# Decode attention with a small MLP on one core: one load queue, a pinned matrix-engine order, a spread-out MLP and a split query-weight load

## The chip, the cores and the metric

The kernel runs on one core of a Trainium2 chip. The metric is the device time of one execution in microseconds (us). A kernel that was timed several times is given by its median. The profile of one execution is shown beside it; its span, from the first to the last instruction, is 1.7 to 2.6 us (1.8 in the median) shorter than the device time of the same execution.

Engine names: PE is TensorE's matmul, PEld its weight load, DVE is VectorE, ACT is ScalarE, POOL is GpSimd, SP is SyncE, which only issues transfers here. PSUM is the memory that PE writes its results to. A packet is one piece of a transfer as the profile's DMA records list it. The granted clock is TensorE's clock as a share of full speed, as the profile page gives it.

## The reference

One token, 16 query heads, 8 K/V heads, 65,536 cached positions of 256 values in bfloat16. The cache is 537 MB and every byte is used once. A small token-mixing MLP and a sigmoid gate are added.

```python
def _A_ref(x, k_cache, v_cache, wq, wo):        # x: (1, 1, 448)
    q = (x @ wq).reshape(B, Sq, 16, 256)...      # wq: (448, 4096)
    k, v = repeat(k_cache, 2), repeat(v_cache, 2)   # (1, 8, 65536, 256) each
    p = softmax(einsum("bhqd,bhkd->bhqk", q, k) * 256 ** -0.5)
    return einsum("bhqk,bhkd->bhqd", p, v)... @ wo  # wo: (4096, 448)

def _B_ref(x, w1, b1, w2, b2):
    h = _layernorm(x)                            # 448 values
    u = gelu(einsum("bsd,sf->bdf", h, w1) + b1)  # 448 x 1792
    return einsum("bdf,fs->bds", u, w2) + b2

g = sigmoid((x * gate_w).sum(-1))
return g * a + (1 - g) * b
```

## The kernel before

The cache is worked through in 256 chunks of 2,048 positions: 1 MB of K and 1 MB of V each. Position `p*16 + j` lies on partition `p`, so one partition receives 8 KB in one piece. PE transposes K in 32 blocks of 128 by 128, DVE copies them out of PSUM, PE forms the scores, ACT takes the exponential, DVE transposes it, and PE multiplies it with V. There are 4 K buffers and 5 V buffers. A helper library puts the instructions of each engine into an order and inserts the waits.

K and the query weight are issued by SP, V by ACT:

```python
wqT = big.tile([PX, KCX, HQ * DH], BF16)              # 112 partitions, 4 x 4096
nc.sync.dma_start(out=wqT[:], in_=A_wq.rearrange("(p kc) n -> p kc n", kc=KCX))
# ... (the query projection, then the output weight's load by POOL)

for g in range(HKV):
    pending = None
    for ck in range(n_chunks):
        # ... buffers of this chunk
        nc.sync.dma_start(out=kn[:, :, :], in_=k_src)
        nc.scalar.dma_start(out=vt[:, :, :], in_=v_src)
        # ... 4 x (8 transposes into tps, copy to kT)
        # ... 8 score matmuls of this chunk
        if pending is not None:
            pv_matmuls(pv, *pending)                  # the chunk before
        nc.scalar.activation(out=p_sb[:, :], in_=ps[:, :], func=ACT.Exp, ...)
        nc.vector.tensor_tensor(out=denacc[:], in0=denacc[:], in1=den[:], op=ALU.add)
        nc.vector.transpose(out=pT[:, :], in_=p_sb[:, :])
        pending = (pT, vt, (ck == 0), (ck == n_chunks - 1))
    pv_matmuls(pv, *pending)
    if g == 0:
        mixer_mlp()                                   # the whole MLP, after head 0
    # ... finish of the head: normalize, output projection into a_ps
```

The MLP, in 14 blocks (the first layer's matmuls are in float32):

```python
for blk in range(NF):
    nc.tensor.matmul(u_ps, lhsT=w1_row[0:1, blk*128:(blk+1)*128], rhs=h_row[0:1, :], start=True, stop=False)
    nc.tensor.matmul(u_ps, lhsT=b1_row[0:1, blk*128:(blk+1)*128], rhs=ones_f32[0:1, :], start=False, stop=True)
    # ... ACT copy, 4 DVE operations and a Tanh on 128 x 448
    nc.tensor.matmul(y_ps, lhsT=w2T_t[:, blk, :], rhs=gel_blk, start=(blk == 0), stop=(blk == NF - 1))
```

The softmax here doesn't subtract the row's maximum and nothing guards it: scores larger than these inputs give would overflow.

## Time and profile before

| | before |
|---|---|
| time, first 4 runs | 1353.27 us median (1352.37 to 1357.23) |
| span of the profiled execution, mean granted clock | 1352.1 us, 0.933 |
| bytes moved, mean rate | 546.37 MB, 404 GB/s |
| PE, DVE, ACT busy | 73%, 65%, 15% |

How to read it: no engine is busy all the time, but the 16 DMA engines nearly are (90% or more in 38 of the page's 40 slices). 546.37 MB at 420 GB/s take 1301 us. So 51 us of the span are not explained by the bytes, and the question is where the rate falls below 420.

These are lines of the profile page of before. The last two have 40 equal slices of 33.8 us: the granted TensorE clock in tenths of full speed, and the rate of the loads.

```profile
span 1352.1 us, 33043 instructions
...
PEclk9789997999899999998989999998899999999988
...
GB/s 281 397 419 419 419 420 325 358 419 420 420 420 419 420 419 420 419 420 420 419 416 419 413 420 413 418 413 413 420 419 418 417 419 417 420 409 412 419 420 178
```

The rate is 419 or 420 in most slices. It is low in the first two, in slices 7 and 8 (325 and 358), a little in some slices after the twentieth (413, 409), and in the last.

Two lines of the table of waits of before say who waits for the loads (total us, times, longest).

```profile
PEld L295 <- DMA kn<-in_A_k_cache_dram: 326.4, 226, 3.0
...
PE tps L295 <- DMA kn<-in_A_k_cache_dram: 225.2, 178, 2.8
```

PE waits for K some 200 times. The loads are the limit, and engine work matters where it holds buffers back. That is the case at 210 us. The columns of the next windows are: from and to; length; busy us of PE, PEld, DVE, ACT and POOL with instruction counts; granted clock; busy share of the DMA engines; GB/s. The two lines under them are from the groups of instructions (line, engine, operation, shapes, count; busy us, mean ns of one; idle before).

```profile
210.00:220.00 10.00, 10.00 (x50) 4.29 (x48) 7.45 (x16) 2.80 (x7) 0.00 (x0) 0.61 0.94 373
220.00:230.00 10.00, 9.67 (x82) 5.50 (x81) 6.03 (x10) 1.79 (x4) 0.00 (x0) 0.71 0.62 236
230.00:240.00 10.00, 10.00 (x79) 4.67 (x78) 7.67 (x18) 2.80 (x6) 0.00 (x0) 0.66 0.76 284
240.00:250.00 10.00, 8.32 (x114) 5.46 (x111) 8.29 (x17) 1.95 (x5) 0.00 (x0) 1.00 0.79 286
250.00:260.00 10.00, 9.60 (x160) 6.39 (x158) 8.86 (x17) 1.83 (x5) 0.00 (x0) 1.00 0.97 388
```

```profile
L224 PE MATMUL oo_ps<-ones_f,b_row 1*128 1x448 f32 x28 | 16.9, 691 | 0.0
L220 PE MATMUL oo_ps<-h_row,w_row 1*128 1x448 f32 x28 | 16.7, 681 | 0.0
```

The MLP's first layer in before is these 28 float32 matmuls (two per block, each recorded twice, so 56 records) of 0.68 to 0.69 us a record. From 210 to 240 us PE is busy 9.67 to 10.00 of 10 us at a clock of 0.61 to 0.71, SP's next loads wait for PE's transposes to free a K buffer (55.3 us in nine waits from 205 to 260 us, the longest 13.4), and the loads fall to 236 GB/s. The start has another cause. These lines are the DMA issues of before (count, KB of each transfer, median us to landing) and the first windows.

```profile
kn<-in_A_k_cache_dram SPq DMA_DIRECT2D x256, 1024.0 KB, 16.5
wqT<-in_A_wq_dram SPq DMA_DIRECT2D x1, 3584.0 KB
```

```profile
0.00:10.00 10.00, 0.24 (x4) 0.21 (x4) 2.80 (x7) 2.46 (x4) 6.47 (x20) 1.00 0.86 253
10.00:20.00 10.00, 0.00 (x0) 0.00 (x0) 0.93 (x3) 0.52 (x2) 0.00 (x0) 1.00 1.01 249
20.00:30.00 10.00, 3.58 (x129) 3.50 (x129) 0.55 (x4) 0.00 (x0) 1.72 (x1) 1.00 0.92 292
30.00:40.00 10.00, 7.17 (x71) 5.89 (x71) 5.60 (x15) 1.97 (x3) 0.00 (x0) 0.90 1.01 403
```

From 10 to 20 us the DMA share is 1.01 and the rate only 249 GB/s: the DMA engines work, but slowly. The packet records show why: the query weight travels in packets of 32 KB that take 2.1 us each, where a K or V packet of 8 KB takes 0.314 us. Last, the windows of before around the end of the loads:

```profile
1326.00:1330.00 4.00, 3.01 (x44) 2.54 (x45) 1.39 (x3) 0.69 (x2) 0.00 (x0) 0.79 0.92 381
1330.00:1334.00 4.00, 3.71 (x56) 2.44 (x55) 2.80 (x7) 0.58 (x2) 0.00 (x0) 0.79 0.51 205
1334.00:1338.00 4.00, 2.77 (x50) 1.83 (x48) 2.47 (x6) 0.22 (x3) 0.00 (x0) 1.00 0.27 113
```

At 1330 us the DMA share is 0.51 at 205 GB/s: half of the DMA engines have nothing left to do while the other half still load (in the packet records, some 8 packets are in flight in place of 16).

### The profile page before, as it was taken

To read this page: it belongs to the slowest core of one execution; us is meant where nothing else is said; L and a number is where in the kernel's file an instruction comes from. 1 tells how busy PE (TensorE), PEld (TensorE's weight loads), DVE (VectorE), ACT (ScalarE), POOL (GpSimd) and SP (SyncE) were. 2 spreads that over 40 slices of the span, in tenths; PEclk is the share of its full clock that TensorE was granted. 3 is DMA by queue.
4 is the path that set the end of the run, shared out by engine and by line. 5 is a ranking of instruction groups with operands and counts; after the bars stand their busy time and mean duration, and the time that the engine had idled before them with its cause. 6 is when DMAs were issued, how large, how long until landed. Compare 5 with 4: busy or idle time off the path is not lost. (4 is left out here: it accounts for less than half of the span.)

```text
span 1352.1 us, 33043 instructions
## 1 busy us (share of the span) xinstructions
PE 990.4 (73%) x14602; PEld 658.2 (49%) x14602; DVE 877.1 (65%) x1665; ACT 196.7 (15%) x554; POOL 8.2 (1%) x21
## 2 busy tenths in 40 slices
PE   2787789877787677767677676777768767777676
PEld 2454555555454445445455444545545444544443
DVE  1576787866666666666666666666666666666665
ACT  0111122111111111111111111111111111111111
POOL 2000000000000000000000000000000000000000
PEclk9789997999899999998989999998899999999988
DMA  9999998999999999999999999999999999999994
GB/s 281 397 419 419 419 420 325 358 419 420 420 420 419 420 419 420 419 420 420 419 416 419 413 420 413 418 413 413 420 419 418 417 419 417 420 409 412 419 420 178
DMA packets 75281, 546.37 MB, mean 404 GB/s; under 512 B 8657, under 2 KB 8674, under 8 KB 9490
## 3 DMA queue, kind: packets, MB, share of 16 engines
q1 hardware_dynamic: 37250, 272.12, 49.2%
q10 hardware_dynamic: 36864, 268.45, 48.3%
q0 software_dynamic: 1024, 3.69, 0.7%
q8 instruction: 114, 1.87, 0.6%
q14 instruction: 29, 0.24, 0.0%
HBM read 544.22 MB, written 0.00 MB: 403 GB/s over the span
## 5 line engine op out<-in xcount | busy, mean ns | idle before, releaser
L300 DVE COPY kT<-tps 128x1024 bf16<-128x1024 bf16 x1024 | 675.0, 681 | 431.6 <-PE tps L295 424.3
L295 PE MATMUL tps<-ident,kn 128*128 128x128 bf16 x8192 | 648.4, 229 | 329.1 <-DMA kn<-in_A_k_cache_dram 225.2
L295 PEld LDWEIGHTS <-kn 128*128 128x128 bf16 x8192 | 509.8, 103 | 553.0 <-DMA kn<-in_A_k_cache_dram 326.4
L319 ACT ACTIVATE p_sb<-sc_ps 128x512 bf16<-128x512 f32 x256 | 152.9, 597 | 1060.8 <-issue 697.2
L308 PE MATMUL sc_ps<-kT,qT_sb 128*2 128x512 bf16 x2048 | 230.2, 399 | 0.8 <-DVE kT L300 0.6
L260 PE MATMUL pv_ps<-vt,pT 128*2 128x256 bf16 x4096 | 213.1, 291 | 2.5 <-DVE pv_sb L336 1.7
L326 DVE STREAM_TRANSPOSE pT<-p_sb 128x512 bf16<-128x512 bf16 x256 | 179.7, 704 | 0.0
L260 PEld LDWEIGHTS <-pT 128*2 128x2 bf16 x4096 | 93.4, 85 | 47.2 <-DVE pT L326 7.5
L308 PEld LDWEIGHTS <-qT_sb 128*2 128x2 bf16 x2048 | 61.0, 82 | 48.7 <-issue 8.9
L319 ACT ACTIVATION_READ_ACCUMULATOR p_sb<-sc_ps 128x1 f32 x256 | 49.8, 194 | 0.0
L323 DVE TENSOR_TENSOR denacc<-denacc,den 128x1 f32<-128x1 f32 x256 | 38.0, 148 | 5.1 <-ACT p_sb L319 5.1
L224 PE MATMUL oo_ps<-ones_f,b_row 1*128 1x448 f32 x28 | 16.9, 691 | 0.0
L220 PE MATMUL oo_ps<-h_row,w_row 1*128 1x448 f32 x28 | 16.7, 681 | 0.0
L174 PE MATMUL misc_ps<-xT,wqT 112*128 112x1 bf16 x128 | 3.6, 165 | 16.5 <-DMA wqT<-in_A_wq_dram 16.5
L174 PEld LDWEIGHTS <-wqT 112*128 112x128 bf16 x128 | 3.5, 104 | 16.6 <-DMA wqT<-in_A_wq_dram 16.6
L229 ACT COPY u_blk<-oo_ps 128x448 f32<-128x448 f32 x14 | 7.4, 527 | 20.0 <-PE oo_ps L224 11.6
L362 PE MATMUL misc_ps<-wo_sb,oT_sb 128*1 128x448 bf16 x32 | 9.0, 377 | 0.0
L237 ACT ACTIVATE t_blk<-t_blk 128x448 f32<-128x448 f32 x14 | 8.0, 572 | 6.9 <-DVE t_blk L236 5.9
L236 DVE TENSOR_TENSOR t_blk<-t_blk,u_blk 128x448 f32<-128x448 f32 x14 | 8.6, 614 | 0.2
L231 DVE TENSOR_TENSOR t_blk<-u_blk 128x448 f32<-128x448 f32 x14 | 8.6, 611 | 0.2 <-ACT u_blk L229 0.2
L193 DVE BATCH_NORM_STATS2 stats<-xB 1x6 f32<-1x448 f32 x1 | 0.6, 615 | 12.4 <-DMA xB<-in_A_x_dram 12.4
L239 DVE SCALAR_TENSOR_TENSOR gel_blk<-t_blk,u_blk 128x448 bf16<-128x448 f32 x14 | 8.3, 612 | 0.0
(58 smaller groups left out, 66.3 us busy)
## 6 DMA issues: line engine op xcount, KB each, us to landing
vt<-in_A_v_cache_dram ACTq DMA_DIRECT2D x256, 1024.0 KB, 16.2
kn<-in_A_k_cache_dram SPq DMA_DIRECT2D x256, 1024.0 KB, 16.5
wqT<-in_A_wq_dram SPq DMA_DIRECT2D x1, 3584.0 KB
wo_sb<-in_A_wo_dram POOLq DMA_DIRECT2D x1, 3584.0 KB, 44.4
xT<-in_A_x_dram SPq DMA_DIRECT2D x1, 0.9 KB, 3.0
gwT<-in_gate_w_dram SPq DMA_DIRECT2D x1, 0.9 KB, 5.7
xB<-in_A_x_dram POOLq DMA_DIRECT2D x1, 1.8 KB, 12.4
w_row<-in_B_w_dram POOLq DMA_DIRECT2D x1, 7.0 KB, 17.2
```

What stands on the lines that cost most here:

```text
L220: nc.tensor.matmul(u_ps[:, :], lhsT=w1_row[0:1, blk * 128:(blk + 1) * 128], rhs=h_row[0:1, :], start=True, stop=False,)
L224: nc.tensor.matmul(u_ps[:, :], lhsT=b1_row[0:1, blk * 128:(blk + 1) * 128], rhs=ones_f32[0:1, :], start=False, stop=True,)
L231: nc.vector.tensor_tensor(out=t_blk[:], in0=u_blk[:], in1=u_blk[:], op=ALU.mult)
L236: nc.vector.tensor_tensor(out=t_blk[:], in0=t_blk[:], in1=u_blk[:], op=ALU.mult)
L260: nc.tensor.matmul(pv[32 * grp:32 * grp + 2, :], lhsT=pT[:, 32 * bcol:32 * bcol + 2], rhs=vt[:, bcol, :], start=first, stop=last, tile_pos ...
L295: nc.tensor.transpose(tp[:, jj * 128:(jj + 1) * 128], kn[:, j, c * 128:(c + 1) * 128], ident[:, :],)
L300: nc.vector.tensor_copy(out=kT[:, c, j0:j0 + 8, :], in_=tp[:, :].rearrange("p (j n) -> p j n", j=8))
L308: nc.tensor.matmul(ps[32 * a:32 * a + 2, :], lhsT=qT_sb[:, c, 2 * g:2 * g + 2], rhs=rhs, start=(c == 0), stop=(c == 1), tile_position=(0, ...
L319: nc.scalar.activation(out=p_sb[:, :], in_=ps[:, :], func=ACT.Exp, scale=inv_sqrt_dh, accum_out=den[:, 0:1],)
L323: nc.vector.tensor_tensor(out=denacc[:], in0=denacc[:], in1=den[:], op=ALU.add)
L326: nc.vector.transpose(out=pT[:, :], in_=p_sb[:, :])
L362: nc.tensor.matmul(a_ps[:, :], lhsT=oT_sb[:, c, h:h + 1], rhs=wo_sb[:, kc, :], start=first, stop=last,)
```

## The change

The intent: let nothing disturb the loads. (1) The query weight goes in four transfers with rows of 8 KB. (2) V moves to SP's queue behind K, 4 chunks ahead; V gets 6 buffers and the transposed K 3. (3) The loop is rewritten so that PE's order is stated and pinned: transposes of the next chunk, scores of this one, PV of the one before. (4) The MLP's first layer folds weight and bias into one matmul of two rows, and its 14 blocks are spread over the first 112 chunks. Sums that stayed open in PSUM for the whole run are now added up by DVE.

```diff
-NKT = 2
-NVBUF = 5
+NKT = 3
+NVBUF = 6
+PREF = 4
@@ the query weight
-    nc.sync.dma_start(
-        out=wqT[:], in_=A_wq.rearrange("(p kc) n -> p kc n", kc=KCX)
-    )
+    for kc in range(KCX):
+        nc.sync.dma_start(
+            out=wqT[:, kc, :], in_=A_wq.rearrange("(p kc) n -> p kc n", kc=KCX)[:, kc, :]
+        )
@@ the loads of a chunk, now in dma_chunk(n)
-            nc.scalar.dma_start(out=vt[:, :, :], in_=v_src)
+        nc.sync.dma_start(out=vt[:, :, :], in_=v_src)
@@ the MLP's first layer, now in mixer_u(blk); w1b1 holds both rows, the second row of h1 is ones
-                u_ps[:, :], lhsT=w1_row[0:1, ...], rhs=h_row[0:1, :], start=True, stop=False,
-                u_ps[:, :], lhsT=b1_row[0:1, ...], rhs=ones_f32[0:1, :], start=False, stop=True,
+            u_ps[:, :], lhsT=w1b1[0:2, blk * 128:(blk + 1) * 128],
+            rhs=h1[0:2, :], start=True, stop=True,
@@ its second layer, now in mixer_y(blk)
+            start=True, stop=True,
+        nc.vector.tensor_tensor(out=y_acc[:], in0=y_acc[:], in1=y_ps[:, :], op=ALU.add)
@@ the loop
+    for n in range(min(PREF, total_chunks)):
+        dma_chunk(n)
+    transposes(0)
+    gate_and_q()
...
+        with tc.manual_schedule(engines={mybir.EngineType.PE}):
+            for n in range(n0, n1):
+                if n + 1 < total_chunks:
+                    transposes(n + 1)
+                scores(n)
+                if last is not None:
+                    pv_stage(last)
+                softmax_stage(n)
+                if n >= 4 and n % 8 == 4 and n // 8 < NF:
+                    mixer_u(n // 8)
+                if n >= 6 and n % 8 == 6 and n // 8 < NF:
+                    mixer_y(n // 8)
+                last = n
+                if n + PREF < total_chunks:
+                    dma_chunk(n + PREF)
```

## The prediction

> **What bounds the kernel now.** The load stream. The profile page: 546 MB moved, mean 404 GB/s over 1352.1 us, nearly all of the 40 slices at 416 to 420 GB/s; PE busy 73%, DVE 65%, ACT 15%. PE waits for K (326 us in the table of waits). At a steady 419.5 GB/s the bytes take 1302 us, so 50 us is lost (table by stretch, packet records):
>
> - 0 to 25 us: 200 to 300 GB/s with the engines busy. The query weight goes as 32 KB packets of 2.1 us (15.5 GB/s per engine); 8 KB packets take 0.314 us (26 GB/s). Lost with the late first byte: 10 us.
> - 40 to 80 us: 398 GB/s beside the output projection's 4.5 KB packets: 2.4 us.
> - 210 to 260 us: 236 to 388 GB/s, 12.7 us. PE is busy 10.0 of 10 us at a granted clock of 0.61 to 0.71: the MLP's 56 fp32 matmuls (0.69 us each) bunch up, K buffers come free late, the queue starves.
> - End: half of the DMA engines run dry 8 us before the others (200 GB/s, 4 us lost), then 15 us of work follow the last landing.
>
> **What the change does.**
> 1. Query weight in four transfers with 8 KB rows: estimated 7 us saved, on the critical path.
> 2. MLP spread over 112 chunks, first-layer matmuls halved: 19 us of PE work and the pile-up gone, 10 to 12 us saved.
> 3. PE's order pinned, the next chunk's transposes ahead of the scores. From the trace's durations (copy 0.65, eight transposes 0.55, scores 0.64, exp with read 0.8, small transpose 0.7 us) I estimate 4.3 us per chunk at full clock, against 5.0 us for its 2 MB. But MLP blocks add 3.3 us per 8 chunks and each head's finish 5 us of PE waiting in line; there compute and loads are nearly level. I allow 3 us of loss.
> 4. K and V on one queue. [...] microseconds in which one queue alone carried data reach 401 to 451 GB/s; an issue costs 0.33 us against 2.5 us per transfer. Neutral.
> 5. Tail: same finish (8 us from the last PV) plus one 0.6 us addition; only V's last 2.5 us lies behind the last K. Estimated 12.5 us.
>
> **Sum.** First byte 3 + bytes and end skew 1306 + projection 2.4 + residual start 1 + tail 12.5 + MLP allowance 3 = 1328 us. From above: 1353 - 7 - 12 - 2.5 - late dips 1 + 3 = 1333. I predict 1328 us, range 1317 to 1342: faster by over 2% 0.40, within 2% 0.55, slower 0.05.
>
> **What would show it.** About 420 GB/s throughout, with no dip near 210 us; query-weight packets at 0.31 us; the half-speed drain of 8 us at the end.
>
> **What would make it wrong.** One queue slower than two (uniformly below 419 GB/s). Low clock in the first half: [...] this trace grants 0.61 during the MLP[...]. Better if the drain at the end vanishes.

Two passages are cut from this text, and marked: the ground that point 4 gave first, and what a lower clock was feared to do. No term of the sum is cut: it came to 1328 us as it stands.

## More of the kernel before

The next lines, from the page of before, list the DMA queues: packets, MB, and the time that the packets took as a share of 16 engines' span.

```profile
q1 hardware_dynamic: 37250, 272.12, 49.2%
q10 hardware_dynamic: 36864, 268.45, 48.3%
...
q8 instruction: 114, 1.87, 0.6%
```

K is on q1 and V on q10.

## The result, and the profile after

| | before | after |
|---|---|---|
| time, runs on the same chip | 1353.58 us (16 runs, 1349.84 to 1357.23) | 1338.27 us (10 runs, 1337.24 to 1338.97) |
| ratio, 95% interval | 1 | 0.9883 (0.9870 to 0.9895) |
| span of the profiled execution, clock | 1352.1 us, 0.933 | 1334.9 us, 0.957 |
| mean rate | 404 GB/s | 409 GB/s |
| PE, DVE busy | 73%, 65% | 68%, 69% |

A ratio is the mean time of one kernel's runs over the mean of the other's runs in the same rounds, so it is not quite the ratio of the medians. The change gains 1.2%: 1338.27 us lies within the predicted range, 10 us above the predicted 1328.

The same lines of the page as before, now of after (a slice is 33.4 us):

```profile
span 1334.9 us, 32973 instructions
...
PEclk9798998999899989999999999999999999999999
...
GB/s 317 411 420 419 420 420 419 420 419 419 420 419 421 419 419 420 419 419 420 419 409 420 419 417 421 409 420 419 413 420 413 420 420 419 411 414 419 416 419 175
```

The dip in slices 7 and 8 is gone and the first two slices are better (317, 411). The late slices still have their 409 to 414, and the last slice is no better. The queues, and the waits for K, in after:

```profile
q1 hardware_dynamic: 74498, 540.58, 98.3%
...
q8 instruction: 113, 1.85, 0.6%
```

```profile
PEld L184 <- DMA kn<-in_A_k_cache_dram: 338.7, 211, 4.8
PE tps L184 <- DMA kn<-in_A_k_cache_dram: 269.4, 197, 4.3
```

One queue carries everything at the same 419 to 420 GB/s. PE waits for K no less than before (338.7 us, 269.4 us), although the kernel is faster, which would fit that it has less work of its own (PE busy 904 us in place of 990) and reaches the wait earlier. A wait at the limiting resource is no measure of what is lost. The windows of after at the same place, and the group of the MLP's first layer:

```profile
210.00:220.00 10.00, 6.60 (x117) 4.87 (x115) 6.79 (x13) 1.38 (x4) 0.00 (x0) 0.99 1.01 419
220.00:230.00 10.00, 7.77 (x78) 4.75 (x79) 6.96 (x13) 1.80 (x4) 0.00 (x0) 0.67 1.02 421
230.00:240.00 10.00, 8.86 (x139) 6.52 (x132) 7.24 (x14) 1.94 (x6) 0.00 (x0) 0.83 1.01 419
```

```profile
L343 PE MATMUL oo_ps<-h,w1b 2*128 2x448 f32 x28 | 14.3, 590 | 0.0
```

28 records of 0.59 us in place of 56, and the loads stay at 419 to 421 GB/s. The start and the end of after:

```profile
wqT<-in_A_wq_dram SPq DMA_DIRECT2D x4, 896.0 KB, 10.3
```

```profile
10.00:20.00 10.00, 2.50 (x81) 2.34 (x82) 2.75 (x13) 0.20 (x1) 0.00 (x0) 1.00 1.02 281
20.00:30.00 10.00, 7.69 (x124) 6.50 (x120) 5.58 (x10) 0.35 (x1) 1.72 (x1) 1.00 1.01 411
```

```profile
1310.00:1314.00 4.00, 2.31 (x43) 1.53 (x43) 2.92 (x6) 0.69 (x2) 0.00 (x0) 1.00 0.58 240
1314.00:1318.00 4.00, 3.10 (x56) 2.20 (x54) 2.75 (x6) 0.69 (x2) 0.00 (x0) 1.00 0.50 205
1318.00:1322.00 4.00, 1.40 (x23) 1.28 (x24) 1.69 (x3) 0.00 (x0) 0.00 (x0) 1.00 0.35 141
```

The slow start ends some 8 us sooner (411 against 292 GB/s from 20 to 30 us; the packet records below have 28 us against 36). The end has the same shape at 205 GB/s, and lasts longer.

To add this up, the packet records were summed by stretch, and each stretch's bytes were set against 419.8 GB/s, the steady rate. "Lost" is the time of the stretch less the time its bytes take at that rate. The clock of the packet records reads 10.3 to 10.6 us more than the span's, so "60 us" here is about 49.5 us in the windows above. "Drain" is from the moment half of the DMA engines run dry (8 packets in flight in place of 16) to the last packet.

```text
lost us         start  60 to  82 to  275 to  600 to  drain         all   rest of the span
                (-60)   82    275    600    drain  (its length)          (before the first and
                                                                          after the last packet)
before          10.2   1.1   12.7    0.1     5.1    4.9 (8.7)    34.1    16.5
after            6.1   0.1    0.1    0.3     4.7    6.8 (12.4)   18.1    15.3
```

The span fell by 17.2 us: 12.6 at the MLP, 4.1 at the start and 1.0 just after it, 0.2 in the middle and late stretches together, 1.2 outside the loads (the tail after the last packet 2.0 shorter, the first packet 0.8 later), and 1.9 were given back in the drain.

### The profile page after: what moved, and what is told of

The parts are those of the page before. It is cut to its first block, busy times and chain, and to the rows that moved or that the text cites. A ratio compares the mean times of both kernels' runs of the same rounds, so it can differ in the third digit from the quotient of the medians.

```text
span 1334.9 us, 32973 instructions
## 1 busy us (share of the span) xinstructions
PE 904.3 (68%) x14574; PEld 643.2 (48%) x14574; DVE 915.2 (69%) x1689; ACT 198.2 (15%) x554; POOL 8.2 (1%) x21
## 5 line engine op out<-in xcount | busy, mean ns | idle before, releaser
L184 PE MATMUL tps<-ident,kn 128*128 128x128 bf16 x8192 | 609.6, 226 | 394.8 <-DMA kn<-in_A_k_cache_dram 269.4
L189 DVE COPY kT<-tps 128x1024 bf16<-128x1024 bf16 x1024 | 662.2, 684 | 210.8 <-PE tps L184 187.6
L184 PEld LDWEIGHTS <-kn 128*128 128x128 bf16 x8192 | 505.4, 101 | 535.0 <-DMA kn<-in_A_k_cache_dram 338.7
L237 PE MATMUL pv_ps<-vt,pT 128*2 128x256 bf16 x4096 | 162.9, 281 | 1.1 <-DVE pT L224 0.8
L201 PE MATMUL sc_ps<-kT,qT_sb 128*2 128x512 bf16 x2048 | 162.8, 396 | 0.0
L237 PEld LDWEIGHTS <-pT 128*2 128x2 bf16 x4096 | 98.8, 87 | 79.0 <-issue 11.6
L201 PEld LDWEIGHTS <-qT_sb 128*2 128x2 bf16 x2048 | 26.3, 79 | 28.6 <-issue 4.5
L343 PE MATMUL oo_ps<-h,w1b 2*128 2x448 f32 x28 | 14.3, 590 | 0.0
L282 DVE TENSOR_TENSOR a_sum<-a_sum,misc_ps 1x448 f32<-1x448 f32 x8 | 4.9, 608 | 6.4 <-PE misc_ps L278 6.4
L253 PE MATMUL oo_ps<-pv_sb,E_f 128*2 128x257 f32 x16 | 4.8, 378 | 5.1 <-ACT pv_sb L251 5.1
## 6 DMA issues: line engine op xcount, KB each, us to landing
kn<-in_A_k_cache_dram SPq DMA_DIRECT2D x256, 1024.0 KB, 17.2
wqT<-in_A_wq_dram SPq DMA_DIRECT2D x4, 896.0 KB, 10.3
```

Source lines behind the costliest of these rows:

```text
L184: nc.tensor.transpose(tp[:, jj * 128:(jj + 1) * 128], kn[:, j, c * 128:(c + 1) * 128], ident[:, :],)
L189: nc.vector.tensor_copy(out=kT[:, c, j0:j0 + 8, :], in_=tp[:, :].rearrange("p (j n) -> p j n", j=8))
L201: nc.tensor.matmul(ps[32 * a:32 * a + 2, :], lhsT=qT_sb[:, c, 2 * g:2 * g + 2], rhs=rhs, start=(c == 0), stop=(c == 1), tile_position=(0, ...
L237: nc.tensor.matmul(pv[32 * grp:32 * grp + 2, :], lhsT=pT[:, 32 * bcol:32 * bcol + 2], rhs=vt[:, bcol, :], start=first, stop=last, tile_pos ...
L343: nc.tensor.matmul(u_ps[:, :], lhsT=w1b1[0:2, blk * 128:(blk + 1) * 128], rhs=h1[0:2, :], start=True, stop=True,)
```

## The experiments

Twelve kernels were run. Each was timed beside before on the same chip; after itself was not run again, so a difference to after is one of ratios to before, and differences of medians are given beside it. About 2 us between such kernels is not a clear difference. The losses of all runs, in the same form as above, are these (free order is left to its own section):

```text
lost us            start  60 to  82 to  275 to  600 to   drain         all   rest
                   (-60)   82    275    600     drain  (length)
before_split        9.8   1.0   12.0    0.2     5.0    4.6 (8.1)     32.7   16.5
before_spread       9.9   1.0    0.2    1.7     5.0    4.7 (8.0)     22.5   20.4
after_bunch         6.4   0.1    4.7   10.4     2.9    6.7 (12.3)    31.1   14.2
after_two_queues   12.0   0.6    0.3    2.0     5.5    3.1 (6.0)     23.5   17.1
after_q128          4.2   0.3    0.2    0.2     4.8    6.9 (12.2)    16.5   18.1
after_q112_rows     7.3   0.0    0.2    0.2     4.9    6.8 (12.1)    19.5   14.9
after_w2_contig     6.6   0.1    0.1    0.6     4.2    6.8 (12.6)    18.4   15.7
after_fewer_pe      6.5   0.1    0.0   -0.1     2.0    6.3 (12.1)    14.8   16.4
after_thin_pv       6.2   0.0    0.1    0.4     5.5    6.0 (10.7)    18.3   16.1
after_wo_8rows      5.8   0.2   20.5    0.7     4.7    8.3 (11.5)    40.2   15.5
after_pv_pairs      7.1   0.0    0.0    0.8     2.5    6.3 (11.5)    16.8   19.0
```

### before_split: the query weight's split alone

```diff
-    nc.sync.dma_start(
-        out=wqT[:], in_=A_wq.rearrange("(p kc) n -> p kc n", kc=KCX)
-    )
+    for kc in range(KCX):
+        nc.sync.dma_start(
+            out=wqT[:, kc, :], in_=A_wq.rearrange("(p kc) n -> p kc n", kc=KCX)[:, kc, :]
+        )
```

> The kernel before with one part of the change: the query weight in four transfers of 8 KB rows. The prediction's term said 7 us. The trace after the change puts the loss of the first 50 us at 6.1 us against 10.2 us before, so the revised theory says 4 us faster (about 1349.5 us), query-weight packets near 0.43 us instead of 2.06 us for four times the bytes, and the dip at 220 to 275 us still there at about 12.7 us lost. Rival (the start is hidden, all of the gain comes from the MLP and the order): within 1 us of the kernel before.

Measured: 1354.29 us, ratio 0.9997 (0.9980 to 1.0015). The split alone gains nothing, and that is a miss. The start loses 9.8 us against 10.2. In the packet records the weight's packets are now 8 KB, but they take 0.42 to 0.5 us, not 0.314. And V's packets, on the other queue, take 0.45 to 0.53 us as well while the weight is in flight. The weight, which needs its 3.7 MB moved in any case, stays in flight until 38 us, and from 16 us on the mean rate is near 270 GB/s.

### before_spread: the MLP's spreading alone

```diff
-        if g == 0:
-            mixer_mlp()
+            if chunk_idx % 8 == 4 and chunk_idx // 8 < NF:
+                mixer_block(chunk_idx // 8, h_row)
+            chunk_idx += 1
@@ needed for it: the open sums of MLP and output projection are closed and added by DVE
+        nc.vector.tensor_tensor(out=y_acc[:], in0=y_acc[:], in1=y_ps[:, :], op=ALU.add)
+        nc.vector.tensor_tensor(out=a_sum[:], in0=a_sum[:], in1=a_ps[:, :], op=ALU.add)
```

> The kernel before with another part alone: the MLP's 14 blocks spread one per 8 chunks (still two fp32 matmuls per block, two queues, scheduler's order, old start). If the bunching of the MLP is the cause of the dip, the dip at 220 to 275 us goes and the kernel is 10 to 12.6 us faster, about 1342 us. Rival (the gain needs the pinned order of PE and the single queue with its fixed prefetch): less than 4 us faster, with dips elsewhere. If the engine skew theory holds (half of the DMA engines carry more bytes, and a dip lets them catch up), the half-speed drain at the end grows from about 8 us to about 12 us, and eats 2 us of the gain.

Measured: 1345.43 us, ratio 0.9932 (0.9918 to 0.9946), 8.4 us by the medians. The matmuls are all still there (two per block), the order is not pinned, V has its own queue: the spread by itself takes the loss from 82 to 275 us from 12.7 to 0.2. Of that, 1.6 us come back in the middle, and the stretch before and after the loads is 3.9 us longer in this profiled execution. So the MLP's part of the gain needs neither the pinned order nor the folded matmul.

### after_bunch: the MLP packed together again, in after

```diff
-                if n >= 4 and n % 8 == 4 and n // 8 < NF:
-                    mixer_u(n // 8)
-                if n >= 6 and n % 8 == 6 and n // 8 < NF:
-                    mixer_y(n // 8)
+                if 32 <= n < 32 + NF:
+                    mixer_u(n - 32)
+                if 33 <= n < 33 + NF:
+                    mixer_y(n - 33)
```

> The kernel after with the MLP bunched again: one block per chunk in chunks 32 to 45, everything else as it is. A chunk with a block needs an estimated 8 to 9 us against 5.0 us of loads, so 14 of them fall some 45 us behind, of which the transfers in flight cover about 15: about 30 us slower than after (1360 to 1370 us), with the load rate at about half in 170 to 300 us and the drain at the end shorter than 13 us if the skew theory holds (about 10 us). Rival (the single queue and pinned order absorb it): within 5 us of after.

Measured: 1350.94 us, ratio 0.9970 (0.9951 to 0.9989), 12.7 us above after by the medians. The direction is as expected, the size is less than half. Three of the windows of after_bunch:

```profile
250.00:260.00 10.00, 6.83 (x78) 4.40 (x76) 8.77 (x17) 2.37 (x5) 0.00 (x0) 0.83 0.90 330
...
270.00:280.00 10.00, 7.00 (x81) 4.57 (x79) 8.77 (x17) 2.21 (x6) 0.00 (x0) 0.83 0.79 299
280.00:290.00 10.00, 8.45 (x94) 4.84 (x93) 8.47 (x17) 2.70 (x8) 0.00 (x0) 0.83 0.83 309
```

With one block per chunk a chunk takes 7 us (2.1 MB at 300 GB/s) in place of 5. The rate is low for only some 65 us, and the losses of 82 to 600 us sum to 15.1 us against 0.4 in after. Both directions of the experiment agree: 8 to 13 us of the result are the MLP's. The limit is not the same in both: in the dip of before PE had no time left at a clock of 0.61 to 0.71, while here DVE (8.2 to 8.8 of 10 us) is busier than PE (6.8 to 8.6). What counts is the pile-up, not one engine.

### after_two_queues: V back on ACT's queue

```diff
-        nc.sync.dma_start(out=vt[:, :, :], in_=v_src)
+        nc.scalar.dma_start(out=vt[:, :, :], in_=v_src)
```

> The kernel after with the V transfers issued from ACT's queue again. The prediction called the single queue neutral: within 2 us of after (1336 to 1340 us), drain at the end still about 13 us[...]. Rival (the single queue causes the longer drain, two queues had 8 us): drain back to 8 us and about 2 us faster; or (the single queue is part of the gain) 3 us or more slower.

Measured: 1343.40 us, ratio 0.9915 (0.9899 to 0.9932), 5.1 us above after by the medians and 4.3 by the ratios. The prediction called one queue neutral; it is not, and the start is where it matters. The start loses 12.0 us against 6.1, while the middle runs at 419 to 420 GB/s. (In this profiled execution the drain was 6.0 us long and lost 3.1, in place of 6.8, but 275 us to the drain lost 2.5 us more than in after, and the rest of the span 1.8.) The first windows of after_two_queues, to be set against 281 and 411 GB/s of after:

```profile
10.00:20.00 10.00, 0.19 (x1) 0.10 (x1) 2.24 (x12) 0.20 (x1) 0.00 (x0) 1.00 1.03 237
20.00:30.00 10.00, 0.37 (x2) 0.21 (x2) 0.00 (x0) 0.00 (x0) 0.00 (x0) 1.00 1.02 273
```

The packet records show the same as in before_split. When does the slow stretch end?

```text
                    queues   weight     rate while the weight    slow until   start
                             packets    flies, from 16 us on     (records)    lost us
before              2        32 KB      206 to 277 GB/s          36 us        10.2
before_split        2         8 KB      183 to 315 GB/s          38 us         9.8
after_two_queues    2         8 KB      169 to 294 GB/s          45 us        12.0
after               1         8 KB      116 to 314 GB/s          28 us         6.1
```

(The rates are of 2 us each, with a packet's bytes spread over the time that it took.) On a single queue the weight goes before K and V, and it is done at 28 us. On two queues V is in flight at the same time, and V's packets are slow for as long as that lasts (0.45 to 0.53 us in before_split, where 0.312 is the steady figure). So the gain at the start belongs to the split and the single queue together: the split without the queue gave nothing (before_split), the queue's loss with the split is 5.9 us of start (this run). The single queue with the weight unsplit was not run. This run and before_spread were timed in the same rounds and both have two queues and a spread MLP: 1343.40 and 1345.43 us. What lies between them (pinned order, folded layer, split weight, buffers) is worth 2.0 us together.

For the steady stream the number of queues made no difference: 419 to 420 GB/s with one and with two. For a slow transfer beside a fast one it did: with the same split weight, the slow stretch ended at 28 us on one queue and at 45 us on two.

### after_q128, after_q112_rows, after_w2_contig: why are the weight's packets slow?

Three candidates: rows that are apart in memory (each partition reads rows `4p+kc`, so one transfer takes every fourth row), 112 partitions in place of 128, and the second-layer weight that POOL loads in pieces of a few bytes at the same time.

```diff
@@ after_q112_rows: partition p reads row kc*112 + p
-        nc.sync.dma_start(out=xT[:], in_=A_x[0, 0].rearrange("(p kc) -> p kc", kc=KCX))
+        nc.sync.dma_start(out=xT[:], in_=A_x[0, 0].rearrange("(kc p) -> p kc", kc=KCX))
 (gate_w and A_wq in the same way)
@@ after_q128: 384 rows on 128 partitions, then 64 rows on 64
-    wqT = big.tile([PX, KCX, HQ * DH], BF16)
+    wqT = big.tile([128, KCX, HQ * DH], BF16)
+    for kc in range(3):
+        nc.sync.dma_start(out=wqT[:, kc, :],
+            in_=A_wq[0:384, :].rearrange("(p kc) n -> p kc n", kc=3)[:, kc, :])
+    nc.sync.dma_start(out=wqT[0:64, 3, :], in_=A_wq[384:448, :])
 (x, gate_w and the matmuls' partition counts in the same way)
@@ after_w2_contig: 28 bytes in one piece per partition
-            out=w2T_t[:, :, :], in_=B_w2.rearrange("(b p) o -> p b o", p=128)
+            out=w2T_t[:, :, :], in_=B_w2.rearrange("(p b) o -> p b o", b=NF)
-            u_ps[:, :], lhsT=w1b1[0:2, blk * 128:(blk + 1) * 128],
+            u_ps[:, :], lhsT=w1b1[0:2, :].rearrange("r (p b) -> r b p", b=NF)[:, blk, :],
```

> The kernel after with the query weight still over 112 partitions, but each transfer reads 112 adjacent rows, one contiguous block, in place of every fourth row (the token and the gate follow the same order). Theory (partition count): packets stay at about 0.43 us, time within 1.5 us of after, perhaps 1 us worse from the 2-byte pieces of the token. Rival (source stride): packets at about 0.32 us and about 3 us faster.

> The kernel after with the query weight laid over 128 partitions (three transfers of 128 rows and one of 64) in place of 112, same rows of 8 KB. Packets of the query weight took about 0.43 us where K's take 0.314. Theory [...]: the packets of the three full transfers take about 0.32 us, the 64-row one stays slow, the start loses about 2 us less, total about 1336 us. Rival (the stride between rows of the source makes them slow): still about 0.43 us and no gain.

> The kernel after with the MLP's second weight loaded as one 28-byte piece per partition in place of 14 pieces of 2 bytes (the hidden columns are permuted to match). In after the load rate falls to 121 to 250 GB/s for about 4 us just when this transfer runs, in before as well. Theory (the 1792 tiny pieces hold up every engine): that notch goes, about 2 us faster, 1336 us. Rival (the notch comes from something else, as the end of the query weight): no change.

Measured: after_q112_rows 1338.71 us (0.9900, 0.9884 to 0.9916), after_q128 1337.46 us (0.9890, 0.9872 to 0.9908), after_w2_contig 1336.31 us (0.9884, 0.9868 to 0.9899). None differs clearly from after's 0.9883. What they tell is in the packet records:

- Neighbouring rows are no faster (0.44 to 0.53 us per packet, start loss 7.3 us). The stride of the source is ruled out.
- On 128 partitions the first two transfers run at 401 and 394 GB/s (16 to 18 and 18 to 20 us of the records), and their packets take 0.31 us in the median. The third slows down to 194 and 190 GB/s from 21 to 23 us, where small packets of POOL's queue (96 and 128 bytes) are in flight, and is back at 369 GB/s in the next microsecond; these are the packets that go with the notch of the next point. The transfer to 64 partitions takes 0.6 us per packet at 209 to 217 GB/s, half of the steady rate. The start loss falls to 4.2 us, but the first packet comes 1.4 us later, with four small loads ahead of it in place of two.
- With the small pieces gone, the notch in after at 22 to 24 us of the records (116 GB/s, packets of 1.1 us) is gone too, but the rest of the start was slower than in after (249 to 275 GB/s; why, is open), and the sum is 6.6 us. No gain is shown.

So the number of the destination's partitions matters, packet by packet: 0.31 us on 128, 0.38 to 0.5 on 112, 0.6 on 64. As rates that is 401 and 394 GB/s on 128 partitions, 293 to 352 in after on 112 (2 us each, 14 to 22 us of the records), and 209 to 217 on 64. Why the number of partitions matters is not shown: the records carry neither the engine nor the place that a packet writes.

### after_wo_8rows: transfers of 8 rows to one half of the partitions, then to the other

The output weight is moved into SP's queue in 16 transfers of 8 rows, one per chunk. The first eight go to partitions 0 to 63, the other eight to partitions 64 to 127. Size, count and packet sizes are equal in both halves (256 packets of 896 bytes per transfer, where the one transfer of after has packets of 4.5 KB). The expectation began from an assumption about the DMA engines that such a transfer uses. The records carry no engine number, so no run shows it. Its "low" and "high" half and the 8 us up or down rested on it alone.

```diff
-    nc.gpsimd.dma_start(
-        out=wo_sb[:], in_=A_wo.rearrange("(kc p) n -> p kc n", p=128)
-    )
+    wo_src = A_wo.rearrange("(kc p) n -> p kc n", p=128)
@@ in the loop
+                if 3 <= n < 19:
+                    p0 = 32 * ((n - 3) // 4) + (n - 3) % 4
+                    nc.sync.dma_start(out=wo_sb[p0:p0 + 29:4], in_=wo_src[p0:p0 + 29:4])
```

> The kernel after with the output projection (3.67 MB) loaded in 16 transfers of 8 rows each from the queue of K and V, one per chunk in chunks 3 to 18, in place of one transfer of 128 rows. [...] Theory (one half is ahead all along and idles 23 us in dips and drain): if the half that is ahead is the low one, dips and drain shrink from 11.8 to about 3 us lost and the kernel is up to 8 us faster (about 1330 us); if it is the high one, 8 us slower with a drain or dips grown by as much. Rival (no fixed half is ahead): within 2 us of after.

Measured: 1358.63 us, ratio 1.0040 (1.0022 to 1.0059), 20 us above after. The windows of after_wo_8rows:

```profile
60.00:70.00 10.00, 7.17 (x119) 5.31 (x118) 7.38 (x14) 1.38 (x4) 0.00 (x0) 0.96 1.02 417
70.00:80.00 10.00, 5.47 (x98) 3.73 (x95) 6.36 (x12) 1.38 (x4) 0.00 (x0) 1.00 1.02 416
80.00:90.00 10.00, 6.70 (x88) 5.65 (x88) 5.28 (x9) 0.69 (x2) 0.00 (x0) 0.83 0.99 395
90.00:100.00 10.00, 6.81 (x88) 4.14 (x86) 5.08 (x10) 1.81 (x5) 0.00 (x0) 0.83 0.99 375
100.00:110.00 10.00, 6.95 (x84) 5.24 (x83) 7.10 (x13) 1.36 (x4) 0.00 (x0) 0.66 1.04 346
110.00:120.00 10.00, 6.02 (x88) 3.60 (x85) 5.84 (x11) 1.38 (x4) 0.00 (x0) 0.83 1.00 322
120.00:130.00 10.00, 5.28 (x64) 3.97 (x65) 3.45 (x6) 0.69 (x2) 0.00 (x0) 0.78 0.92 297
```

In the packet records the first five transfers (67 to 95 us, 410 to 422 GB/s) lose 0.5 us together, and K and V packets stay at 0.312 us. The sixth to eighth, still to partitions 32 to 63, lose 1.9 us, in short dips in which a few K and V packets take 0.8 to 2.0 us. From the ninth on (117 us), to partitions 64 to 127, each transfer loses 1.7 to 2.9 us: while it flies the rate is mostly 234 to 280 GB/s, and most K and V packets take 0.5 to 0.6 us. These eight lose 17.5 us for 1.8 MB that need 4.4 us; all of 82 to 275 us loses 20.5. The run had been made to see whether extra work on one half of the engines shortens or lengthens the drain at the end. It can't tell that, as the second half of its transfers disturbs everything. But it is the clearest sign here that it matters which partitions a transfer writes, since only the destination and the place in the run differ between the halves. The place is not ruled out, as the loss begins with the sixth transfer. Why the transfers to partitions 64 to 127 are the slow ones is not shown.

### after_free_order: PE's order not pinned

```diff
-        with tc.manual_schedule(engines={mybir.EngineType.PE}):
+        if True:
             for n in range(n0, n1):
```

> The kernel after without the pinned order of PE: the scheduler orders PE's instructions by itself. Theory (loads bound the kernel from 60 us on and compute has slack, so the order is worth nothing by itself): within 2 us of after, 1336 to 1340 us, no dip over 3 us lost between 82 and 600 us. Rival (the pinned order keeps the loads going): 5 us or more slower, with dips.

Measured: 1786.71 us, ratio 1.3204 (1.3176 to 1.3232). I had expected within 2 us: a large miss. The first line is from the page of after_free_order, the second from its waits:

```profile
GB/s 340 410 310 307 309 282 320 293 318 307 281 331 315 311 305 318 295 319 296 319 306 307 311 306 308 306 314 299 316 304 306 314 312 301 312 307 306 308 310 89
```

```profile
PE pv_ps L237 <- DVE pT L224: 388.1, 242, 1.9
```

In after the same wait is 0.8 us for the whole run. Left to itself, the library puts the PV matmuls of a chunk right behind that chunk's own scores. PE then waits 1.6 us in 242 of 256 chunks for scores, exponential and transpose to come back, and a chunk takes 7 us in place of 5, at 306 GB/s. The mean granted clock fell to 0.804. Before runs without a pin; its source emits the PV of the chunk before ahead of the exponential, which is the likely reason (not tested). So the pin has no gain over before to show (at most a part of the 2.0 us between before_spread and after_two_queues), but the rewritten loop can't do without it.

### after_fewer_pe and after_thin_pv: the late dips and the drain

From about 690 us on (in after_two_queues from about 370), all kernels that keep the loads busy have short dips to 400 to 414 GB/s, and at the end half of the DMA engines run dry early. From 275 us to the end they lose 10.1 us in before, 11.8 in after, 11.4 in before_spread and 10.6 in after_two_queues: the change did not touch this loss. A suspect is q8, the queue of instructions. It carries 113 packets of 16 KB in after, and a packet takes 1.07 us. In each kernel their number is that of PE's instructions (weight loads and matmuls) divided by 256: 2 x 14,574 / 256 = 113.9. In before it is 2 x 14,602 / 256 = 114.1 for 114 packets, in after_pv_pairs below 2 x 12,526 / 256 = 97.9 for 98. Which DMA engines carry q8 is not in the records; that they are the half that ends last is a theory of the expectations and was not shown.

Two kernels tell the fetch from PE's work. Both give a wrong result: one drops 12 of 16 PV matmuls, the other keeps them all but takes 32 of 256 columns. (The comparison with the reference passed nonetheless: its tolerance does not see this part of the output.)

```diff
@@ after_fewer_pe
-        for bcol in range(NJ):
+        for bcol in range(4):  # wrong result on purpose: 4 of 16
@@ after_thin_pv
-                pv[32 * grp:32 * grp + 2, :],
+                pv[32 * grp:32 * grp + 2, 0:32],
-                rhs=vt[:, bcol, :],
+                rhs=vt[:, bcol, 0:32],  # wrong result on purpose: 32 of 256 columns
```

> The kernel after with 12 of the 16 PV products of each chunk left out (a wrong result on purpose; all loads stay). PE's instructions fall by 24 of about 114 per chunk, 21%. At the end half of the DMA engines drain 12 us later than the others, and the fetch of PE's instructions (1.87 MB in 16 KB packets of 1.07 us, 122 us in all) would be 15 us for each of 8 engines. Theory (that fetch sits on one half of the engines): fetched bytes 1.5 MB, the late dips and the drain together lose about 1.6 us less, total about 1336.5 us. Rival 1 (the skew has another source): dips and drain lose the same 11.8 us together and the time stays at 1338. Rival 2 (PE's work itself limits): several us faster.

> The control for after_fewer_pe: all 16 PV products of a chunk stay, but each takes 32 of the 256 columns (a wrong result on purpose), so PE does less work with the same number of instructions to fetch. after_fewer_pe was 5.8 us faster than after, and its late dips fell from 4.7 to 2.0 us lost. Theory (fetch of PE's instructions): here the fetched bytes stay at 1.85 MB, dips and drain stay near 11.8 us lost together, and the time stays within 1.5 us of after (about 1337 us, a shorter tail included). Rival (PE's work): as fast as after_fewer_pe, about 1332.5 us, dips near 2 us.

The queue of instructions in after_fewer_pe, and then in after_thin_pv:

```profile
q8 instruction: 90, 1.47, 0.5%
```

```profile
q8 instruction: 114, 1.87, 0.6%
```

Measured: after_fewer_pe 1332.39 us (0.9854, 0.9838 to 0.9870), 5.9 us below after by the medians and 3.9 by the ratios; after_thin_pv 1337.98 us (0.9893, 0.9871 to 0.9914), the same as after. Less PV work with the same instruction count (PV matmuls busy 70.6 us in after_thin_pv, 162.9 in after) changes nothing; fewer instructions do. With 23 packets fewer the dips lose 2.0 us in place of 4.7, and the loads end 4.3 us sooner. So the fetch of instructions is a part of the late loss: an estimated 0.19 us for each packet (4.3 us / 23), where 16 KB at 419.8 GB/s would be 0.04. One rival is left: after_fewer_pe also drops the weight loads of its matmuls, which after_thin_pv keeps. The next run, with 16 packets fewer and all products kept, speaks for the fetch. The drain's length hardly moved (12.1 us). Why half of the engines end later than the others, and why the drain is 8.7 us in before and 12.4 in after, stays open.

### after_pv_pairs: fewer instructions with a right result

Two PV matmuls are joined into one with 34 stationary columns and 512 moving ones. The cross terms that it computes as well are ignored.

```diff
-        for bcol in range(NJ):
-            grp = bcol % 4
+        for pair in range(NJ // 2):
+            grp = pair % 2
...
-                pv[32 * grp:32 * grp + 2, :],
-                lhsT=pT[:, 32 * bcol:32 * bcol + 2],
-                rhs=vt[:, bcol, :],
+                pv[64 * grp:64 * grp + 34, :],
+                lhsT=pT[:, 64 * pair:64 * pair + 34],
+                rhs=vt[:, 2 * pair:2 * pair + 2, :],
@@ finish of a head: four copies of 32 partitions in place of one
-        nc.scalar.copy(out=pv_sb[:, 0:DH], in_=pv[:, :])
+        for a in range(4):
+            p, c0 = slice(32 * a, 32 * a + 32), DH * (a % 2)
+            ...
```

> The kernel after with two neighbouring PV products in one: 8 matmuls of 34 stationary columns and 512 moving ones per chunk in place of 16 of 2 and 256 (the right result; the same products are kept, the unwanted blocks are never read). PE has 4,096 instructions fewer, 12 to 14%, which is about 16 packets of 16 KB fewer to fetch. after_fewer_pe had 23 packets fewer and was 5.8 us faster. Theory (the fetch of PE's instructions rides on the half of the DMA engines that ends last): in proportion about 3.8 us faster than after, 1334.4 us, fetched bytes about 1.6 MB, late dips from 4.7 to about 3 us lost, the drain near its 12 us. Rival (it was the work left out): within 1 us of after, or slower [...].

(The reason for "or slower" is cut; what was measured of it stands below.)

The queue of instructions in after_pv_pairs:

```profile
q8 instruction: 98, 1.61, 0.5%
```

Measured: 1338.63 us, ratio 0.9890 (0.9867 to 0.9912), the same as after: a miss. The loads do end sooner (dips 2.5 us in place of 4.7, data 1.9 us shorter in spite of a start that lost 1.0 us more), which supports the fetch. But the tail got longer. In the timelines, from the last K transpose to the issue of the output, after takes 9.9 us and this kernel 12.9: a chunk's PV takes 1.04 us in place of 0.61, the copies out of PSUM 1.6 us in place of 0.4, and both lie in line at the end. No version was found that clearly beats after with a right result. The lowest median was after_w2_contig's 1336.31 us, with the same ratio as after. Joined versions were not run.

## Why the prediction was right or wrong

The outcome, within 2% and near 1% faster, and the range of 1317 to 1342 us were right. The point, 1328, was 10 us too low. Point by point:

- **"The load stream" bounds the kernel, and what counts is where it loses:** right. PE's and DVE's work changed (PE 73% to 68%, DVE 65% to 69%), and the gain is where the rate rose; after_thin_pv, with less PV work still (70.6 us in place of 162.9), gained nothing more.
- **MLP "10 to 12 us saved":** right in mechanism and nearly in size: 12.6 us less lost in that stretch. before_spread and after_bunch show it from both sides, at 8.4 and 12.7 us.
- **"I allow 3 us of loss" for MLP blocks and heads' finish:** not needed, 82 to 600 us lose 0.4 us in all. The feared loss from a low clock did not come either: the clock sinks to 0.67 from 220 to 230 us, where the loads run at 421 GB/s.
- **Query weight "7 us saved", packets "at 0.31 us":** wrong in both. They take 0.38 to 0.46 us in after (medians of the four transfers), and 4.1 us were saved at the start. The step that failed is that a packet of 8 KB costs the same whatever its destination: on 112 partitions it is slower than on 128 (0.31 us in after_q128). The 1.0 us saved from 60 to 82 us belongs to another term, the output projection's load: it was in flight until 81 us of the records in before and lost 2.0 us, and until 62 us in after and lost 0.9. The prediction left its 2.4 us unchanged.
- **K and V on one queue: "Neutral":** wrong. It is neutral in the steady state, but with V on the other queue the start loses 5.9 us more and the time rises by about 5. The split alone gains nothing. The prediction credited the split with what only split and queue order bring together.
- **"Half-speed drain of 8 us":** the drain was 12.4 us. And the dips were costed at 1 us saved, where they did not change.
- **Tail "12.5 us" after the last landing:** right, 12.6 us, from 14.6 in before.
- **PE's order, 4.3 us per chunk:** the pinned order holds the loads at 420 GB/s, right in effect; what a chunk would take without the loads' limit was not measured. I had not seen that without the pin the same loop takes 7 us per chunk.

The sum shows which term was mis-sized. The profiled execution took 1336.75 us:

```text
term                                   predicted   measured   from
first byte                                3           2.7     15.3 outside the loads, less the tail
bytes                                  1302        1301.5     546.35 MB at 419.8 GB/s
late dips and drain ("end skew")          4          11.5     4.7 + 6.8
start and projection                      3.4         6.2     6.1 + 0.1
MLP allowance                             3           0.4     0.1 + 0.3
tail after the last landing              12.5        12.6
device time outside the span              0           1.85    1336.75 - 1334.9
sum                                    1327.9      1336.75
```

The largest error is the end skew: the prediction counted the drain alone, at 4 us, and overlooked that before already lost 5.1 us in the late dips. The estimate from above (1333), which began from the measured 1353, carried those losses along without knowing them, and came nearer. That the start's 2.8 us too little and the allowance's 2.6 us too much cancel is luck.

Shown by runs: the MLP's part, the joint effect of split and queue, the need for the pin, and that packets to 112 partitions are slower than to 128. Shown but for the rival named there: the part of the instruction fetch. Not shown: why packets to 112 partitions are slower. Open: which half of the engines ends later, the longer drain, and why the rest of the start of after_w2_contig was slower.

## What to carry to other kernels

When the loads are the limit, sum the lost time by stretch against the steady rate, count every stretch that is even 2% low, and predict from that ledger; here waits and busy shares did not show the gain. A slow transfer cost here as long as it was in flight beside the others (12.0 us lost at the start on two queues, 6.1 on one), so send it first on the common queue, and spread any burst of engine work so that buffers come free in time (12.7 us lost with the MLP in one piece, 0.2 with it spread). (128 partitions made the packets of the first transfers faster, but no gain in time is shown: 1337.46 against 1338.27 us.) Test each part of a change alone and also taken out of the whole: the split weight was worth nothing by itself, and the pinned order had no clear gain over before but was worth 450 us to the new loop.
